# Two of sixteen weight loads cut into 24, 24 and 80 rows, with two eight-row transfers in between

## The chip, the core and the metric

The kernel runs on one core of one Trainium2 chip. TensorE (PE) multiplies matrices and transposes, VectorE (DVE) and ScalarE (ACT) work on vectors, GpSimd (POOL) and SyncE (SP) mostly issue transfers. Transfers from the chip's main memory (HBM) into the core's memory (SBUF) are moved by 16 DMA engines that all queues share. The metric is the time of one execution on the device in microseconds (us), the median of several executions.

## The reference

Two stages. First an attention over 4 batches, 8 heads, 768 positions and 64 columns a head; three heads see all earlier positions, five see the first 4 positions and a window of 64. Then a mixture of experts with soft slots: 32 slots take weighted means of all 3072 rows of the attention's result, 8 experts with two weight matrices each (512 x 1024 and 1024 x 512) work on four slots each, and every row gets a weighted mean of the slots' results.

```python
x = attn_out.transpose(0, 2, 1, 3).reshape(B * S, H * D)   # 3072 x 512
logits = x @ phi                                           # 3072 x 32
slot_input = softmax(logits, over rows).T @ x              # 32 x 512
for e in range(8):
    h = relu(slot_input[e] @ w1[e])                        # 4 x 1024
    slot_out[e] = h @ w2[e]                                # 4 x 512
out = softmax(logits, over slots) @ slot_out
```

## The kernel before

**Loads.** q, k and v of the four batches and the 16 weights (numbers 0 to 7 are w1 of the experts, 8 to 15 are w2) are read from HBM as 4-byte numbers and written to SBUF as 2-byte numbers, a conversion made by the transfer itself. All of these loads are issued by POOL, through `dma` (lines 329 to 337), and stand in its one queue, q0. A load of q, k or v of batches 1 to 3 (`load_part`, line 347) has 96 rows, each of two 4 KB pieces as written; one of a weight (`load_w`, line 385) has 128 rows, each of two 4 KB pieces. Batch 0 is loaded in halves (384 KB each), weights 14 and 15 in column halves (`load_half`, line 381). The order of the calls is the order of the queue: batch 0, w0, batch 1, w1, w2, batch 2, w3 to w5, batch 3, w6 to w10 (lines 516 to 525), later w11 to w13 and the halves 14.0, 15.0, 14.1, 15.1 (lines 859 to 866). In the views of the transfers, the row of a load gives the KB that it writes and the us from issue to landing.

**Memory for the loads.** Eleven slots (`slots`, line 246) take q, k, v and the weights 0 to 10. A slot in which a q, k or v lay is free again when TensorE has transposed it (line 566); a weight stays. The weights 11 to 15 go to memory that the attention no longer needs.

**The order of the work.** The program is laid out by a list scheduler (`Plan`, lines 33 to 149). Every operation has its engine, an estimated duration, what it depends on, the buffers that it takes and frees, and a due time (its key); the planner repeatedly takes the operation that can start first, and the one with the lowest key among those within 0.12 us of it. `SHIFTS` (line 167) is a list of changes of due times for the operations between two keys; the loads, with key -100, are not among them. Instructions of an engine run in the planned order. The issue of a load is an operation on POOL; it waits for the issue before it and, by lines 330 and 331, for the landing of the eighth load before it. The estimated landing is an operation on a made-up engine called DMA. POOL also makes a few tables, and three copies of exponentials (`EL4`, line 801), each of which a transpose on TensorE (line 836) waits for.

**The attention.** For each of the 16 pairs of batch and head group, TensorE transposes q, k and v (line 566), forms scores (line 599), ScalarE takes exponentials (line 668), VectorE applies masks (line 615), TensorE multiplies by v (line 729), and the result is normed (line 750), transposed again (line 762) and used for the logits.

**The experts.** From about 115 us on, TensorE multiplies the slots' means by the weights 0 to 7 (line 904), then the results by the weights 8 to 15 (line 942). The last two, 14 and 15, are used by column halves: halves 14.0 and 15.0 complete the left half of the slots' results, whose rows of the output are formed (line 998), scaled (lines 1006 and 1008) and stored (line 1017) while 14.1 and 15.1 still load; with these the right half follows, and the last stores.

**What the change touches.** `load_w` for the weights 6 and 7 (called at line 525), and the memory of `ident_u` (line 261), a 96 x 96 matrix that the transposes of batch 0 use.

Of the kernel before, what the change touches and what calls it, by code (L numbers as in the profile page):

```python
# [11 lines left out]
BF16 = mybir.dt.bfloat16  # L12
# [3 lines left out]
PSUM = bass.MemoryType.PSUM  # L16
KB = 512
PAD = 16


class Buf:
# [194 lines left out]
def kernel(  # L216
# [14 lines left out]
    P = 128  # L231
# [3 lines left out]
    NS = moe_phi.shape[1]  # L235
# [4 lines left out]
    sb = ctx.enter_context(tc.tile_pool(name="sb", bufs=1))  # L240
# [4 lines left out]

    slots = [sb.tile([P, 8 * KB + 2 * PAD], BF16, name=f"slot{i}") for i in range(11)]
    qk_mem = [sb.tile([P, 12 * KB], BF16, name=f"qk{i}") for i in range(2)]
# [10 lines left out]
    ssum = sb.tile([P, B], F32, name="ssum")  # L258
    fmx = sb.tile([P, 4, 2, 4, 66], BF16, name="fmx")
    ident = sb.tile([P, P], BF16, name="ident")  # L260
    ident_u = sb.tile([96, 96], BF16, name="ident_u")
    ident_r = sb.tile([P, P], BF16, name="ident_r")
    phf = sb.tile([P, 4, NS], F32, name="phf")
    phi = sb.tile([P, 4, NS], BF16, name="phi")
# [50 lines left out]
    def on(eng, occ, late=0.18):  # L315
        return {eng: (occ, occ + late)}
# [12 lines left out]
    def dma(name, nbytes, buf, dst, src, deps=()):  # L329
        if len(chain) >= 8:  # L330
            deps = list(deps) + [chain[-8]]
        iss = pl.op("issue " + name, on("POOL", 0.645, 1.4), -100, deps=list(deps) + [fifo[0]],
                    acq=[buf] if buf else [], lead=1.3, emit=lambda o: nc.gpsimd.dma_start(dst(), src))  # L333
        fifo[0] = iss
        took = nbytes / 425000.0
        chain.append(pl.op("land " + name, {"DMA": (took, took + 1.3 + min(2.1, 0.22 * len(chain)))}, -100, deps=[iss] + chain[-1:], lead=3.4))
        return chain[-1]
# [25 lines left out]
    wbuf = [Buf("S8") for _ in range(NW)]  # L363
    wland = [None] * NW
    late_mem = {}

    def w_mem(i):

        m = late_mem[i]() if i in late_mem else slots[wbuf[i].slot][:, :]
        return m.rearrange("p (h x) -> p h x", h=2)[:, :, 0:4 * KB]  # L370
# [14 lines left out]
    def load_w(i, deps=()):  # L385
        if i < NE:
            src = moe_w1[i].rearrange("(di h a) f -> di h (a f)", h=2, a=2)
        else:
            src = moe_w2[i - NE].rearrange("(fi h a) d -> fi h (a d)", h=2, a=4)
        wland[i] = dma(f"w{i}", 2 << 20, None if i in late_mem else wbuf[i],  # L390
                       lambda: w_mem(i), src, deps=deps)


    def tables(o):
# [32 lines left out]
    def head_flags(o, n):  # L427
        cp = nc.scalar.copy if o.eng == "ACT" else nc.gpsimd.tensor_copy
        for a, j0, j1 in ((1, 1, 4), (0, 0, 1)):
            cp(fmx[:, n, :, j0:j1, :].rearrange("p i j d -> p i (j d)"),  # L430
               thr[:, a, n::4].rearrange("p (i o) -> p i o", o=1).to_broadcast([P, 2, 66 * (j1 - j0)]))
# [72 lines left out]
    for n in range(4):  # L504
        o_fm[n] = pl.op(f"fm{n}", on("ACT", 0.65) if n == 0 else on("POOL", 0.9), -8 if n == 0 else T * n - 3.5,
                        deps=[o_fl], emit=lambda o, n=n: head_flags(o, n))
# [5 lines left out]
    def batch_loads(b):  # L512
        for x in "qkv":
            load_part(x, b)

    load_w(0)
    batch_loads(1)
    load_w(1)
    load_w(2)
    batch_loads(2)  # L520
    for i in (3, 4, 5):
# [67 lines left out]
    def evs(x, b, n):  # L589
        return ev[x, 0, n // 2] if b == 0 else ev[x, b]  # L590
# [15 lines left out]
    def mask_emit(b, n, g):  # L606
        def f(o):
            pT = pTs[PTb[b, n].slot]
            mh = msk[:, n::4, :]
            if g < 2:  # L610
                pT = pT[:, :, 1024 * g:1024 * (g + 1)].rearrange("p i (a c) -> p i a c", a=2)[:, :, :, 0:256]
                mh = mh[:, :, 256 * g:256 * g + 512].rearrange("p i (a c) -> p i a c", a=2)
            else:
                pT, mh = pT[:, :, 2048:2432], mh[:, :, 256:640]
            nc.vector.tensor_tensor(pT, pT, mh, op=ALU.mult)  # L615
        return f
# [5 lines left out]
    for b in range(B):  # L622
        for n in range(4):
# [29 lines left out]
            for kk, g in enumerate(range(5)):  # L653
# [19 lines left out]
                for m, gs in enumerate(MGROUPS):  # L673
                    if gs[-1] == g:
                        o_m = pl.op(f"MK.{p}.{m}", on("DVE", [0.605, 0.605, 0.47][m]), key + 0.3,
                                    deps=[expo[p, x] for x in gs] + [o_hm[n]], emit=mask_emit(b, n, m))
# [3 lines left out]
        for ns in ([(0, 1), (2, 3)] if b == 0 else [(0, 1, 2, 3)]):  # L680
            sc = Buf("SC")

            def emit_lx(o, b=b, sc=sc, ns=ns):
# [4 lines left out]
                      deps=list(dict.fromkeys(e for n in ns for x in "qk" for e in evs(x, b, n))),  # L688
# [14 lines left out]
    for b in range(B):  # L703
        for n in range(4):
# [5 lines left out]
            for i in iorder:  # L710
                deps, need = [v2e[p], vfo[p]], set()
# [7 lines left out]
                def emit_pv(o, b=b, n=n, p=p, i=i):  # L719
                    pT = pTs[PTb[b, n].slot]  # L720
                    vb = vbs[VBb[b].slot]
                    for h in range(2):
                        for j in range(i + 1):
# [3 lines left out]
                            else:  # L727
# [5 lines left out]
                             deps=list(dict.fromkeys(deps)) + ([last] if last else []),  # L733
# [8 lines left out]
            for i0, i1 in halves:  # L742
                part = f"{p}" if i1 - i0 == 6 else f"{p}.{i0}"

                def emit_nm(o, i0=i0, i1=i1, b=b, n=n, p=p):
# [9 lines left out]
                                 deps=[pvo[i1 - 1], XBb[b].op], acq=[XBb[b]] if n == 0 else [], rel=[PVb[p]],  # L755
# [94 lines left out]

    late_mem[11] = lambda: qk_mem[QTb[2].slot][:, 0:8 * KB + 2 * PAD]
    late_mem[12] = lambda: vx_mem[VBb[2].slot][:, 0:8 * KB + 2 * PAD]
    late_mem[13] = lambda: xv_mem[:, 0:8 * KB + 2 * PAD]
    late_mem[14] = lambda: pt_mem[:, 10 * KB * PTb[3, 2].slot:10 * KB * PTb[3, 2].slot + 8 * KB]
# [233 lines left out]
```

## Time and profile before

| | us |
|---|---|
| time, median of 3 executions | 150.83 (150.63 to 150.85) |
| the profiled execution's own time | 150.88 |
| its span (first to last instruction) | 149.1 |
| TensorE busy | 125.5 |
| VectorE busy | 109.1 |
| ScalarE busy | 107.4 |
| POOL busy | 33.1 |

The profile is of one execution. Its times count from the start of the span; the execution's own time holds the 1.8 us around the span as well. A row of the timeline gives start, duration, engine, line, the tile that is written and what is read, and in brackets how long the engine had been idle before and what ended that. In the slices of the span a digit is the busy share of a fortieth in tenths. The DMA share of a window is the mean number of transfers' pieces in progress per DMA engine, which exceeds 1 where pieces overlap on one engine.

### The profile page before, as it was taken

How to read it: one execution, taken by the hardware profiler on the slowest of the kernel's cores; microseconds unless marked ns; L12 is line 12 of the kernel's file. 1: busy time of each engine (PE TensorE's matmuls, PEld its weight loads, DVE VectorE, ACT ScalarE, POOL GpSimd, SP SyncE). 2: the span in 40 equal slices, each digit the busy share in tenths (PEclk: the TensorE clock that was granted, in tenths of full speed). 3: DMA queues.
4: the chain of work that ended last, by engine and by line, in shares of the span. 5: the costliest groups of instructions: out<-in, count | busy, mean ns of one | idle time of the engine just before them, and what ended most of it. 6: DMA issues, size and time to landing. Idle time of an engine off the chain costs nothing.

```text
span 149.1 us, 5309 instructions
## 1 busy us (share of the span) xinstructions
PE 125.5 (84%) x2351; PEld 85.8 (58%) x2351; DVE 109.1 (73%) x232; ACT 107.4 (72%) x138; POOL 33.1 (22%) x58
## 2 busy tenths in 40 slices
PE   6799987996999999999999997999779994959100
PEld 1297665774776776877667775757565552634000
DVE  1897999966898988999899997998953130749500
ACT  3127899996779999999999997999913530738300
POOL 6996301111111001210210122050630000430000
PEclk9999999999599999999999999999968999586975
DMA  2999999999999999999999999999999999999995
GB/s 21 193 210 210 216 214 215 216 214 213 216 210 215 215 216 218 209 212 218 214 216 212 211 216 219 216 211 212 213 220 215 201 196 198 142 305 336 391 422 209
DMA packets 14263, 32.92 MB, mean 221 GB/s; under 512 B 1376, under 2 KB 7008, under 8 KB 13856
## 3 DMA queue, kind: packets, MB, share of 16 engines
q0 software_dynamic: 11536, 27.79, 95.0%
q1 hardware_dynamic: 2704, 4.79, 8.5%
q8 instruction: 18, 0.29, 0.7%
q14 instruction: 5, 0.04, 0.1%
HBM read 52.50 MB, written 6.29 MB: 394 GB/s over the span
## 4 chain that ended last, share of the span: by engine, by line
PE 48%; DMA 15%; DVE 11%; ACT 8%; issue 7%; POOL 3%; DVEq 1%; POOLq 0%; ACTq 0%
DMA qk<-in_moe_w_dram 15%; PE tr L566 13%; PE sc L599 11%; PE pv L729 11%; ACT pt L668 5%; PE tr L762 3%; PE bk L998 3%; DVE xv L750 2%; PE tr L632 2%; DVE pt L615 2%; PE sc L485 2%; DVE vx L322 1%; ACT qk L320 1%; DVE slot L1008 1%; DVE vf L647 1%
## 5 line engine op out<-in xcount | busy, mean ns | idle before, releaser
L668 ACT ACTIVATE pt<-sc 128x1024 bf16<-128x1024 f32 x80 | 77.4, 1047 | 4.9 <-PE sc L599 4.6
L599 PE MATMUL sc<-qk 64*128 64x128 bf16 (+3 forms) x288 | 32.1, 298 | 1.6 <-ACT pt L668 1.4
L615 DVE TENSOR_TENSOR pt<-pt,msk 128x1024 bf16<-128x1024 bf16 (+1 forms) x48 | 30.1, 639 | 1.5 <-ACT pt L668 1.1
L729 PEld LDWEIGHTS <-pt 128*128 128x128 bf16 x640 | 23.9, 98 | 6.8 <-issue 3.7
L729 PE MATMUL pv<-vx,pt 128*128 128x65 bf16 x352 | 26.9, 194 | 0.1
L566 PEld LDWEIGHTS <-slot 96*64 96x64 bf16 x768 | 20.1, 115 | 7.2 <-issue 5.3
L729 PE MATMUL pv<-vf,pt 128*128 128x65 bf16 x288 | 21.7, 196 | 0.9 <-DVE xv L750 0.9
L566 PE MATMUL tr<-ident,slot 96*64 96x96 bf16 x576 | 18.0, 212 | 1.3 <-issue 1.3
L322 DVE COPY qk<-tr 128x768 bf16<-128x768 bf16 x28 | 14.9, 549 | 4.0 <-PE tr L566 3.9
L599 PEld LDWEIGHTS <-qk 64*128 64x128 bf16 x288 | 11.5, 95 | 9.0 <-issue 3.3
L750 DVE TENSOR_TENSOR xv<-pv,rs 128x768 bf16<-128x768 f32 (+1 forms) x17 | 15.5, 910 | 0.6
L333 POOL DMA_DIRECT2D slot<-in_moe_w_dram x11 | 7.8, 707 | 26.6 <-PE tr L566 19.2
L1006 ACT ACTIVATE slot<-bk,rrow 128x256 f32<-128x256 f32 (+1 forms) x17 | 8.5, 548 | 3.6 <-PE bk L998 3.5
L762 PE MATMUL tr<-ident,xv 128*128 128x128 bf16 x96 | 8.8, 230 | 1.4 <-DVE xv L750 0.9
L1008 DVE TENSOR_SCALAR slot<-bk,rrow 128x256 f32<-128x256 f32 (+1 forms) x19 | 9.3, 561 | 0.6 <-PE bk L998 0.4
L762 PEld LDWEIGHTS <-xv 128*128 128x128 bf16 x96 | 6.2, 102 | 4.9 <-DVE xv L750 2.5
L632 PE MATMUL tr<-ident,xv 128*128 128x128 bf16 x96 | 8.2, 220 | 1.0 <-issue 0.9
L322 DVE COPY xT<-tr 128x768 bf16<-128x768 bf16 (+1 forms) x14 | 7.3, 525 | 2.3 <-PE tr L762 1.3
L998 PE MATMUL bk<-msk,expT 128*128 128x256 bf16 (+1 forms) x36 | 8.4, 413 | 0.7 <-DVE msk L983 0.7
L322 DVE COPY vx<-tr 128x768 bf16<-128x768 bf16 x13 | 7.1, 550 | 1.1 <-PE tr L632 1.0
L632 PEld LDWEIGHTS <-xv 128*128 128x128 bf16 x96 | 5.7, 97 | 3.0 <-issue 2.5
L1017 POOL DMA_DIRECT2D out_dram<-slot x4 | 2.8, 709 | 19.6 <-DVE slot L1008 19.5
(101 smaller groups left out, 152.1 us busy)
## 6 DMA issues: line engine op xcount, KB each, us to landing
slot<-in_moe_w_dram POOLq DMA_DIRECT2D x11, 1024.0 KB, 26.4
out_dram<-slot SPq DMA_DIRECT2D x3, 1024.0 KB, 6.6
slot<-in_q_dram POOLq DMA_DIRECT2D x3, 768.0 KB, 30.4
slot<-in_k_dram POOLq DMA_DIRECT2D x3, 768.0 KB, 32.7
slot<-in_v_dram POOLq DMA_DIRECT2D x3, 768.0 KB, 23.8
out_dram<-slot SPq DMA_DIRECT2D x3, 512.0 KB, 3.7
qk<-in_moe_w_dram POOLq DMA_DIRECT2D x1, 1024.0 KB, 21.3
vx<-in_moe_w_dram POOLq DMA_DIRECT2D x1, 1024.0 KB, 24.0
```

What stands on the lines that cost most here:

```text
L322: nc.vector.tensor_copy(dst, src)
L566: nc.tensor.transpose(dst_, rv[:, i, 8 * c + s, :], idv)
L599: nc.tensor.matmul(scb[sc.slot][:, i, c:c + 128 * nb], kk, qq.rearrange("p b c -> p (b c)"), start=True, stop=True)
L615: nc.vector.tensor_tensor(pT, pT, mh, op=ALU.mult)
L632: nc.tensor.transpose(t[:, 128 * j:128 * (j + 1)], vT[:, 6 * n + j, :], ident)
L668: nc.scalar.activation(pTs[PTb[b, n].slot][:, :, 512 * g:512 * (g + 1)], scb[sc.slot], ACT.Exp, scale=scale)
L729: nc.tensor.matmul(pvb[:, h, 65 * i:65 * (i + 1)], lt, rhs, start=(j == 0), stop=(j == i))
L750: nc.vector.tensor_tensor(xo, pvw[:, :, :, 0:64], r.rearrange("p i (j o) -> p i j o", o=1).to_broadcast([P, 2, i1 - i0, 64]), op=ALU.mult)
L762: nc.tensor.transpose(t[:, 128 * i:128 * (i + 1)], xv[:, i, 128 * n:128 * (n + 1)], ident)
L998: nc.tensor.matmul(banks[bf.slot][:, 0:w], out_lhs(gi, r), slot_out[:, cs], start=True, stop=True)
L1006: nc.scalar.activation(d, banks[bf.slot][:, 0:w], ACT.Copy, scale=sc_)
L1008: nc.vector.tensor_scalar(d, banks[bf.slot][:, 0:w], sc_, None, op0=ALU.mult)
```

## The change

The loads of the weights 6 and 7 are each cut into three, of rows 0 to 23, 24 to 47 and 48 to 127, into the same memory as before. After each of the first two a small transfer is issued: eight rows of 32 numbers from the slots' matrix `phi`, into eight rows of SBUF that nothing else uses. There are four such transfers, each with eight rows of its own, in rows 96 to 127 of a tile that has been made taller for that; rows 0 to 95 hold what `ident_u` held. Two transfers on POOL's queue thus become ten, in the order 24 rows, small, 24 rows, small, 80 rows, for weight 6 and then for weight 7. The first part of a weight takes the slot; all parts go through `dma`, so each of the ten counts for the rule of the eighth load before.

```diff
--- before.py
+++ after.py
@@ -16,6 +16,7 @@
 PSUM = bass.MemoryType.PSUM
 KB = 512
 PAD = 16
+UNEVEN = {6: (24, 0, 24, 0, 80), 7: (24, 0, 24, 0, 80)}
 
 
 class Buf:
@@ -258,7 +259,9 @@
     ssum = sb.tile([P, B], F32, name="ssum")
     fmx = sb.tile([P, 4, 2, 4, 66], BF16, name="fmx")
     ident = sb.tile([P, P], BF16, name="ident")
-    ident_u = sb.tile([96, 96], BF16, name="ident_u")
+    ident_m = sb.tile([P, 96], BF16, name="ident_u")
+    ident_u = ident_m[0:96, :]
+    few = [ident_m[96 + 8 * x:104 + 8 * x, 0:NS] for x in range(4)]
     ident_r = sb.tile([P, P], BF16, name="ident_r")
     phf = sb.tile([P, 4, NS], F32, name="phf")
     phi = sb.tile([P, 4, NS], BF16, name="phi")
@@ -387,8 +390,19 @@
             src = moe_w1[i].rearrange("(di h a) f -> di h (a f)", h=2, a=2)
         else:
             src = moe_w2[i - NE].rearrange("(fi h a) d -> fi h (a d)", h=2, a=4)
-        wland[i] = dma(f"w{i}", 2 << 20, None if i in late_mem else wbuf[i],
-                       lambda: w_mem(i), src, deps=deps)
+        if i not in UNEVEN:
+            wland[i] = dma(f"w{i}", 2 << 20, None if i in late_mem else wbuf[i],
+                           lambda: w_mem(i), src, deps=deps)
+            return
+        rows, p0 = UNEVEN[i], 0
+        for x, n in enumerate(rows):
+            if n == 0:
+                dma(f"gap{i}.{x}", 1024, None, lambda m=few.pop(): m, moe_phi[0:8, :])
+                continue
+            wland[i] = dma(f"w{i}.{p0}", n << 14, wbuf[i] if p0 == 0 else None,
+                           lambda p0=p0, n=n: w_mem(i)[p0:p0 + n], src[p0:p0 + n], deps=deps)
+            p0 += n
+        assert p0 == 128
 
 
     def tables(o):
```

## The prediction

> **What bounds the kernel now.** I read the page first, then the chain that ended last, then POOL's timeline, then the landing of single transfers, then the last microseconds of the loads in short windows.
>
> ```profile
> span 149.1 us, 5309 instructions
> ...
> PE 125.5 (84%) x2351; PEld 85.8 (58%) x2351; DVE 109.1 (73%) x232; ACT 107.4 (72%) x138; POOL 33.1 (22%) x58
> ...
> DMA  2999999999999999999999999999999999999995
> ...
> q0 software_dynamic: 11536, 27.79, 95.0%
> ...
> q8 instruction: 18, 0.29, 0.7%
> ...
> PE 48%; DMA 15%; DVE 11%; ACT 8%; issue 7%; POOL 3%; DVEq 1%; POOLq 0%; ACTq 0%
> ```
>
> TensorE is the busiest engine, but the row to look at is DMA: from the second slice on, the 16 engines are always nine tenths busy or more, nearly all with POOL's queue q0. The chain says where that becomes the end:
>
> ```profile
> 107.56 0.86 POOL pt L333
> 108.43 23.09 DMA qk<-in_moe_w_dram
> 131.56 0.43 PE bk L942 x8
> ```
>
> The last load (second half of weight 15) is issued at 108.43 and lands at 131.5, behind everything queued ahead of it; TensorE starts on it at once. TensorE had to wait there, and before for the first half:
>
> ```profile
> 126.30 0.55 PE L942 MATMUL bk<-qk,xT 128*32 128x256 bf16 x8 [2.03 <-DMA qk<-in_moe_w_dram]
> ...
> 131.56 0.40 PE L942 MATMUL bk<-qk,xT 128*32 128x256 bf16 x8 [1.17 <-DMA qk<-in_moe_w_dram]
> ```
>
> So the time is: end of the load stream at 131.5, plus a fixed tail of 149.1 - 131.5 = 17.6 us, plus 150.88 - 149.1 = 1.8 us outside the span. A later stream costs one to one; an earlier one pays up to about 2.0 us, until TensorE itself is the last (the waits of 2.03 and 1.17 are on consecutive parts of one chain and both move with the stream).
>
> Where the stream ends is not the same for all engines. The last columns of the windows are clock, DMA share and GB/s:
>
> ```profile
> 124.00:127.00 3.00, 0.97 (x28) 0.43 (x17) 0.00 (x0) 0.12 (x1) 0.00 (x0) 0.90 1.45 197
> 127.00:128.00 1.00, 1.00 (x25) 0.84 (x23) 0.31 (x1) 0.36 (x1) 0.00 (x0) 0.50 1.17 165
> 128.00:129.00 1.00, 1.00 (x7) 0.72 (x5) 0.99 (x3) 0.94 (x3) 0.21 (x1) 0.50 0.78 100
> 129.00:130.00 1.00, 1.00 (x9) 0.50 (x8) 1.00 (x4) 1.00 (x3) 0.90 (x2) 0.58 0.70 114
> ```
>
> From 128 on, half the rate is left (100 of 197): about eight engines have finished, eight work on to 130 and 131.5. So there are **early and late engines**, 2 to 3.5 us apart. The q8 row gives a likely cause: 18 instruction fetches take 0.7% of 16 x 149.1 us = 16.7 us, 0.93 us each; shared by eight engines that is 2.1 us per engine. Even engines would end the stream sooner: the rate lost in 127 to 130 is 32 + 97 + 83 = 212 KB, 1.1 us at 197 KB/us, and at most about as much again after 130. This spread is what the change can touch: how many rows each engine gets.
>
> **The change part by part.** (1) The bytes of weights 6 and 7 stay the same. (2) Two transfers become ten on q0: eight more, four of them eight rows of 32 numbers. (3) POOL issues eight more. (4) The eight-back rule (line 330: an issue waits for the landing of the eighth transfer before it) now counts pieces. (5) The 24-row parts can be uneven over the 16 engines. The small rows go to memory that nothing reads.
>
> *Cost of a transfer in the stream (2).* Landings come from issue time plus time to landing. For the seven loads from weight 6 to 13:
>
> ```profile
> 59.87 0.70 POOL L333 DMA_DIRECT2D slot<-in_moe_w_dram  x1
> ...
> 98.72 0.71 POOL L333 DMA_DIRECT2D xv<-in_moe_w_dram  x1 [0.33 <-PE tr L810]
> ```
> ```profile
> slot<-in_moe_w_dram POOLq DMA_DIRECT2D x1, 1024.0 KB, 25.7
> ```
> ```profile
> xv<-in_moe_w_dram POOLq DMA_DIRECT2D x1, 1024.0 KB, 21.1
> ```
>
> 59.87 + 25.7 = 85.57 and 98.72 + 21.1 = 119.82: 34.25 / 7 = 4.89 us for 128 rows, 0.61 us per row of an engine (eight rows each). For 96 rows, the q and v of batch 1 (issued 7.97 and 9.23, two transfers apart):
>
> ```profile
> 7.97 0.66 POOL L333 DMA_DIRECT2D slot<-in_q_dram  x1
> ...
> 9.23 0.66 POOL L333 DMA_DIRECT2D slot<-in_v_dram  x1
> ```
> ```profile
> slot<-in_q_dram POOLq DMA_DIRECT2D x1, 768.0 KB, 17.6
> ```
> ```profile
> slot<-in_v_dram POOLq DMA_DIRECT2D x1, 768.0 KB, 23.8
> ```
>
> 25.57 and 33.03: 3.73 us for six rows each. From 8r + f = 4.89 and 6r + f = 3.73, f = 0.25 us per transfer; but if the time went by rows alone (4.89 / 8 = 0.611 against 3.73 / 6 = 0.622) f is 0 to 0.07. A single fetch of 0.93 us between two landings explains the difference, so I bound f by 0 and 0.15 (no reason lets an added transfer take less than nothing) and take 0.08, nearer to the proportional pair: 8 x 0.08 = **0.64 us**, bounds 0 and 1.2. All engines get this, the late ones too, and nothing hides it.
>
> [...]
>
> *POOL and the eight-back rule (3, 4).*
>
> ```profile
> 12.99 0.72 POOL L333 DMA_DIRECT2D slot<-in_moe_w_dram  x1
> ...
> 33.55 0.70 POOL L333 DMA_DIRECT2D slot<-in_moe_w_dram  x1 [2.96 <-PE tr L566]
> 38.43 0.66 POOL L333 DMA_DIRECT2D slot<-in_q_dram  x1 [4.18 <-PE sc L599]
> 43.39 0.63 POOL L333 DMA_DIRECT2D slot<-in_k_dram  x1 [4.30 <-DMA slot<-in_moe_w_dram]
> ...
> 59.25 0.63 POOL L333 DMA_DIRECT2D slot<-in_v_dram  x1 [10.85 <-PE tr L566]
> ...
> 71.71 0.83 POOL L801 COPY elg<-elg 128x576 bf16<-128x576 bf16 x1 [6.91 <-DMA slot<-in_q_dram]
> ...
> 88.39 0.70 POOL L333 DMA_DIRECT2D slot<-in_moe_w_dram  x1 [4.94 <-PE tr L566]
> ```
> ```profile
> slot<-in_moe_w_dram POOLq DMA_DIRECT2D x1, 1024.0 KB, 29.8
> ```
> ```profile
> slot<-in_moe_w_dram POOLq DMA_DIRECT2D x1, 1024.0 KB, 36.1
> ```
> ```profile
> slot<-in_q_dram POOLq DMA_DIRECT2D x1, 768.0 KB, 35.1
> ```
> ```profile
> slot<-in_v_dram POOLq DMA_DIRECT2D x1, 768.0 KB, 21.4
> ```
>
> The rule is seen at 43.39: weight 2, eighth before k of batch 3, landed at 12.99 + 29.8 = 42.79, and the issue follows 0.60 us later. Eight issues at 0.70 are 5.6 us more of POOL. Now the new order: the third part of weight 6 (80 rows) is eighth after weight 5, which lands at 33.55 + 36.1 = 69.65: issued 70.25 to 70.95. The copy at 71.71 (line 801, which really waits for ScalarE's exponentials, not for the q named) comes next, so it is not delayed, by a margin of 0.76 us; behind it stands the transpose of line 836 on TensorE. Weight 7's first part waits for q of batch 3 (38.43 + 35.1 = 73.53), its second for v (59.25 + 21.4 = 80.65): issued at 81.25; the small transfer behind that for weight 6's first part, some 1.3 us after v, so about 82.6; its third part at 83.3, weights 8 and 9 at 84.0 and 84.7, before 88.39, where weight 10 waits for a buffer as now. I take the order of all other instructions as unchanged, since each added operation finds POOL idle.
>
> Does the stream run dry meanwhile? When v lands at 80.65, weight 6 (4.9 us) and 24 rows of weight 7 (0.9 us) are queued: the late engines have work to 86.5. The third part of weight 7 is issued at 83.3; if it takes 2.5 us to start (an upper bound from the 8 KB load of line 454, whole 2.5 us to landing) it is there at 85.8. So nothing is lost on late engines; the early ones, 2 to 3 us ahead, may idle up to 2 us, which the spread at the end covers. Without that cover every microsecond is paid.
>
> ```profile
> ri<-in_is_retrieval_dram SPq DMA_DIRECT2D x1, 8.0 KB, 2.5
> ```
>
> *Which engines get the rows (5).* No row shows a transfer on POOL's queue other than 96 or 128 rows, both even over 16. Bounds, at 0.61 us a row: the late engines give away two rows of 32 (below) and the stream ends 1.22 us earlier; or they get two more and it ends 1.22 us later. I take the value between, 0, from those two nearest rows: a row is two 4 KB pieces, 24 rows are 48 = 3 x 16 pieces, and over four such parts any dealer that moves on comes round evenly.
>
> [...]
>
> Sum: 150.88 + 0.64 = **151.5** (0 from POOL, 0 from uneven rows). The median shown is 150.83, 0.05 below the profiled execution.
>
> **Rivals.** *Faster: the early engines take more.* If rows are dealt one by one, 16 to a round, 24 rows are a round and a half and the eight small rows fill the half: every 24-row part then starts at the same engine. Eight engines get two rows and eight get one, four times: 8 against 4, where even is 6. If the eight are the early ones, the late ones end 1.22 us sooner: 150.88 - 1.22 + 0.64 = 150.3. For it: 24 + 8 = 32 closes the round exactly, and half the engines are late, with about four rows' time (2.4 us) between the halves. Against: nothing says which half starts.
>
> *Slower: the late engines take more.* The same deal from the other half, or a deal that always begins at the first engine with two rows for each of 12: late engines are then among those with eight rows, 150.88 + 1.22 + 0.64 = 152.7. It decides as soon as one of the latest engines lies in the favoured set. [...]
>
> *Eight engines with three rows each.* With a fixed start these have 6 rows too many, 3.7 us: on the early ones they become the last, about 151.9; on the late ones 155.2.
>
> *Queue or copy.* If parts wait for one another, or weight 5 lands over 0.76 us later, POOL stands still in front of line 801 and the stream dries: 153 and more. Against: the two loads of line 457 go to different rows of one tile, and both are issued within 1.41 us, though each takes 3.9 us to land.
>
> ```profile
> 1.17 1.41 SPq L457 DMA_DIRECT2D phf<-in_moe_phi_dram  x2
> ```
> ```profile
> phf<-in_moe_phi_dram SPq DMA_DIRECT2D x2, 32.0 KB, 3.9
> ```
>
> *No difference*: f near 0 and rows even, 150.9.
>
> **How the numbers follow.** Even rows 0.42 (own range 150.9 to 152.1 by the bounds of f; 0.04 of it within 0.2%), late engines 0.24, early engines 0.20 (0.03 of it within 0.2%), eight engines 0.05, queue 0.04, no difference 0.05. Faster by over 0.2% (about 0.3 us, what a measurement of this kernel can tell): 0.17; within: 0.04 + 0.03 + 0.05 = 0.12; slower: 0.38 + 0.24 + 0.05 + 0.04 = 0.71. The range 150.2 to 152.9 reaches over the first three cases and leaves out the eight-engine and queue cases and the edges.
>
> **What would show it.** Right: the second half of weight 15 lands at about 132.2, its 23.1 us grown by 0.6; the rate still halves near 128.6; line 801 starts near 71.7; the tail stays 17.6 us. Rows even or not is seen in the windows before the last landing: if the rate holds at 197 up to the end, the early engines took more; if it halves earlier and the last landing is near 133.4, the late ones did. Wrong: a wait in front of line 801, DMA shares under 1.0 between 80 and 90, or a gap of 4 us between landings that the small transfers cause.

## The result and the profile after

The changed kernel takes 151.74 us, median of 20 executions (151.1 to 152.86); the kernel before took 151.0 beside it (20 executions, 150.63 to 151.93). The ratio is 1.0044, interval 1.0027 to 1.006: **0.66 us slower**, between 0.41 and 0.91. The forecast was 151.5, or 0.64 more. The size came out nearly as forecast, but not by the way that the forecast gave for it: as far as the number goes, that is luck.

The profiled execution took 151.65 us. The lines of the page of the changed kernel that answer to those of before:

```profile
span 149.9 us, 5320 instructions
...
PE 123.4 (82%) x2351; PEld 83.3 (56%) x2351; DVE 110.3 (74%) x232; ACT 107.8 (72%) x138; POOL 37.4 (25%) x66
...
DMA  2999999999999999999999999999999999997994
...
q0 software_dynamic: 11792, 27.79, 94.8%
...
q8 instruction: 18, 0.29, 0.7%
```

POOL has eight instructions more (66 for 58) and is busy 4.3 us more; q0 moves the same 27.79 MB in 256 more pieces. The other engines have their old counts. The order of all instructions other than these issues is the same on each engine. In the text of the changed kernel the lines of `dma` and of the attention stand 3 to 14 lower: 333 is now 336, 801 is 815, 942 is 956.

The end of the chain that ended last, and TensorE's rows on the last load, in the changed kernel:

```profile
107.24 0.87 POOL pt L336
108.11 23.71 DMA qk<-in_moe_w_dram
131.86 0.64 PE bk L956 x7
```
```profile
126.23 0.40 PE L956 MATMUL bk<-qk,xT 128*32 128x256 bf16 x8 [2.23 <-DMA qk<-in_moe_w_dram]
...
131.86 0.61 PE L956 MATMUL bk<-qk,xT 128*32 128x256 bf16 x8 [1.80 <-DMA qk<-in_moe_w_dram]
```

The bound is the same as before: TensorE waits 1.80 us for the second half of weight 15. That half lands 23.71 us after its issue at 108.11, at 131.82: **0.30 us later than before**, where the forecast had 0.6. From TensorE's start on it to the end of the span are 149.9 - 131.86 = 18.0 us, where before they were 149.1 - 131.56 = 17.5. So of the 0.77 us between the two profiled executions, 0.30 are the stream and **0.47 the tail**, which the forecast took as fixed. These are two single executions; what the tail does in the median isn't shown.

POOL's timeline of the changed kernel (start, duration, engine, line, transfer; in brackets the idle time before and what ended it):

```profile
57.68 0.61 POOL L336 DMA_DIRECT2D slot<-in_moe_w_dram  x1
58.28 0.54 POOL L336 DMA_DIRECT2D ident_u<-in_moe_phi_dram  x1
58.82 0.61 POOL L336 DMA_DIRECT2D slot<-in_moe_w_dram  x1
63.69 0.52 POOL L336 DMA_DIRECT2D ident_u<-in_moe_phi_dram  x1 [4.26 <-DMA slot<-in_moe_w_dram]
69.70 0.64 POOL L336 DMA_DIRECT2D slot<-in_moe_w_dram  x1 [5.49 <-DMA slot<-in_moe_w_dram]
70.33 0.68 POOL L815 COPY elg<-elg 128x576 bf16<-128x576 bf16 x1
73.66 0.60 POOL L336 DMA_DIRECT2D slot<-in_moe_w_dram  x1 [2.64 <-PE tr L580]
77.07 0.53 POOL L336 DMA_DIRECT2D ident_u<-in_moe_phi_dram  x1 [2.81 <-DMA slot<-in_k_dram]
81.36 0.60 POOL L336 DMA_DIRECT2D slot<-in_moe_w_dram  x1 [3.76 <-DMA slot<-in_v_dram]
82.29 0.52 POOL L336 DMA_DIRECT2D ident_u<-in_moe_phi_dram  x1 [0.32 <-DMA slot<-in_moe_w_dram]
82.80 2.20 POOL L336 DMA_DIRECT2D slot<-in_moe_w_dram  x3
88.33 0.70 POOL L336 DMA_DIRECT2D slot<-in_moe_w_dram  x1 [3.33 <-PE tr L580]
```

This is the plan of the forecast nearly to the tenth: 69.70 for a forecast 70.25, 81.36 for 81.25, 82.29 for 82.6, 88.33 for 88.39. The copy (line 815) isn't delayed. Weight 7, one issue at 64.09 before, now has five, from 73.66 to 82.80, because of the rule of the eighth load before, which now counts pieces.

The rates while weights 6 and 7 move (last columns: granted clock, DMA share, GB/s), before and after:

```profile
76.00:80.00 4.00, 4.00 (x100) 2.93 (x100) 3.94 (x8) 3.64 (x5) 0.70 (x1) 1.00 1.07 216
80.00:84.00 4.00, 4.00 (x98) 2.87 (x93) 3.85 (x8) 4.00 (x5) 0.71 (x1) 1.00 1.07 216
84.00:88.00 4.00, 4.00 (x114) 3.20 (x110) 3.87 (x9) 4.00 (x6) 0.00 (x0) 1.00 1.06 213
88.00:92.00 4.00, 3.09 (x58) 2.07 (x54) 3.63 (x7) 3.63 (x5) 2.10 (x3) 1.00 1.07 216
```
```profile
76.00:80.00 4.00, 3.96 (x92) 2.74 (x88) 3.79 (x8) 3.62 (x5) 0.53 (x1) 1.00 1.06 211
80.00:84.00 4.00, 4.00 (x90) 2.93 (x90) 3.92 (x9) 3.87 (x5) 2.31 (x4) 1.00 1.08 208
84.00:88.00 4.00, 3.43 (x98) 2.62 (x96) 3.33 (x7) 3.73 (x5) 0.85 (x2) 1.00 1.06 204
88.00:92.00 4.00, 3.37 (x61) 2.35 (x60) 3.59 (x7) 3.53 (x5) 2.10 (x3) 1.00 1.07 215
```

Before, the rate hardly moves. After, 208 and 204 stand between 80 and 88: 4 x (8 + 9) = 68 KB less, 0.32 us at 213 KB/us, just where the queue lives on pieces issued at 81.36 to 82.80. From 88 on the rate is back. The 211 for 216 between 76 and 80 stands in several kernels below with no piece issued late (210 to 214 there), so 5 GB/s in one window is no more than their scatter.

### The profile page after: what moved, and what is told of

It reads as the page before. It is cut to its first block, busy times and chain, and to the rows that moved or that the text cites. A ratio compares the mean times of both kernels' runs of the same rounds, so it can differ in the third digit from the quotient of the medians.

```text
span 149.9 us, 5320 instructions
## 1 busy us (share of the span) xinstructions
PE 123.4 (82%) x2351; PEld 83.3 (56%) x2351; DVE 110.3 (74%) x232; ACT 107.8 (72%) x138; POOL 37.4 (25%) x66
## 3 DMA queue, kind: packets, MB, share of 16 engines
q0 software_dynamic: 11792, 27.79, 94.8%
## 4 chain that ended last, share of the span: by engine, by line
DMA 39%; PE 37%; DVE 9%; issue 3%; POOL 3%; ACT 2%; DVEq 1%; POOLq 0%
DMA slot<-in_q_dram 23%; DMA qk<-in_moe_w_dram 16%; PE tr L580 9%; PE pv L743 8%; PE sc L613 8%; PE bk L1012 4%; PE tr L776 3%; PE sc L499 2%; DVE pt L629 1%; DVE xv L764 1%; PE tr L646 1%; ACT qk L323 1%; DVE vx L325 1%; POOL slot L336 1%; DVE slot L1022 1%
## 5 line engine op out<-in xcount | busy, mean ns | idle before, releaser
L743 PEld LDWEIGHTS <-pt 128*128 128x128 bf16 x640 | 23.4, 97 | 6.9 <-issue 3.7
L580 PEld LDWEIGHTS <-slot 96*64 96x64 bf16 x768 | 19.3, 112 | 8.4 <-issue 5.0
L743 PE MATMUL pv<-vf,pt 128*128 128x65 bf16 x288 | 21.2, 194 | 0.9 <-DVE xv L764 0.9
L336 POOL DMA_DIRECT2D slot<-in_moe_w_dram x15 | 10.1, 673 | 24.4 <-DMA slot<-in_v_dram 6.5
L776 PE MATMUL tr<-ident,xv 128*128 128x128 bf16 x96 | 8.2, 220 | 1.3 <-DVE xv L764 0.9
L646 PE MATMUL tr<-ident,xv 128*128 128x128 bf16 x96 | 8.2, 220 | 0.7 <-issue 0.6
L776 PEld LDWEIGHTS <-xv 128*128 128x128 bf16 x96 | 5.8, 97 | 4.4 <-DVE xv L764 1.9
L661 DVE TENSOR_TENSOR vf<-vx,fmx 128x528 bf16<-128x528 bf16 x16 | 7.7, 492 | 0.4
```

The source lines that it names most:

```text
L580: nc.tensor.transpose(dst_, rv[:, i, 8 * c + s, :], idv)
L646: nc.tensor.transpose(t[:, 128 * j:128 * (j + 1)], vT[:, 6 * n + j, :], ident)
L743: nc.tensor.matmul(pvb[:, h, 65 * i:65 * (i + 1)], lt, rhs, start=(j == 0), stop=(j == i))
L776: nc.tensor.transpose(t[:, 128 * i:128 * (i + 1)], xv[:, i, 128 * n:128 * (n + 1)], ident)
```

## The experiments

**Theories.** *Count* (the forecast): each added transfer costs every engine about 0.08 us, wherever it stands. *Rows*: the cost is an uneven deal of the 24-row parts over the engines. *Late issue*: the transfers as such are nearly free, but pieces that wait for the eighth piece before them are issued so late that engines run out of work between 82 and 88 us. All kernels below differ from the changed one in `UNEVEN` (rows of each part of a weight; 0 stands for a small transfer) and in `few`, the memory of the small transfers. A difference below is the ratio's, applied to the kernel before as it was measured beside that run (medians 151.1 to 151.2); the plain difference of the two medians departs from it by up to 0.2 us.

*Splits alone.*
```diff
-UNEVEN = {6: (24, 0, 24, 0, 80), 7: (24, 0, 24, 0, 80)}
+UNEVEN = {6: (24, 24, 80), 7: (24, 24, 80)}
```


> The change without its four small transfers: weights 6 and 7 as 24, 24 and 80 rows, four more transfers than before. By the count of transfers (0.08 us each): +0.3 us. By the queue (the late issues of POOL from 81 us on, which came from ten pieces in the eight-back rule, leave engines without work; here the last part is issued at about 73 and weight 8 at 77): +0.0 to +0.2 us.

Measured: 151.16, ratio 0.9998 (0.9979 to 1.0016), -0.03 us for four added transfers.

*Even parts, same count and order.*
```diff
+UNEVEN = {6: (32, 0, 32, 0, 64), 7: (32, 0, 32, 0, 64)}
```


> The change with 32, 32 and 64 rows in place of 24, 24 and 80: the same ten transfers, every part a multiple of 16 rows. By the count of transfers, and by the queue alike (issues from 81 us on as late as in the change): +0.6 us. If the uneven rows are what costs: +0.2 or less.

Measured: 151.54, ratio 1.0023 (1.0009 to 1.0038), +0.35 us: about half of the change's cost, with nothing uneven.

*Splits of four weights, with no, one and two small transfers each.* These ask how rows are dealt: a deal that always starts at the same engine would send four parts too many to it, and small transfers would shift a start that moves.
```diff
+UNEVEN = {i: (24, 24, 80) for i in range(6, 10)}
```


> Weights 6 to 9 as 24, 24 and 80 rows, no small transfers: eight more transfers than before. The theory (rows come out even over the 16 engines, each added transfer takes 0.08 us of every engine): +0.6 us, 151.5. Always the lowest twelve engines with two rows each: they get 4 rows too many (eight parts, half a row each), 2.4 us, so about +3.1 us. Rows dealt one by one: two parts close three rounds, even, +0.6. Twelve engines from a start that moves: one weight favours one half, the next the other, even, +0.6.

Measured: 151.44, ratio 1.0028 (1.0006 to 1.0051), +0.42 us for eight added.
```diff
+UNEVEN = {i: (24, 24, 0, 80) for i in range(6, 10)}
```


> Weights 6 to 9 as 24, 24, a small transfer of eight rows, 80: twelve more transfers. The theory: +1.0 us, rate halves before the end as before. Twelve engines from a start that moves by the engines used: 12 + 12 + 8 = 32, so the same eight engines get a row more and the other eight a row less in each of four weights, 4 rows or 2.4 us each way: about -0.5 to +1 if the early ones take more (they become the last), +3.4 if the late ones do. Rows dealt one by one: even over two weights, +1.0. Always the lowest twelve: +3.4.

Measured: 151.48, ratio 1.0025 (1.0 to 1.0049), +0.38 us for twelve added.
```diff
+UNEVEN = {i: (24, 0, 24, 0, 80) for i in range(6, 10)}
```


> The change's own pattern on four weights, 6 to 9, sixteen more transfers. The theory: twice the change, +1.3 us. Rows dealt one by one from the first engine: eight engines get 4 rows more than even, eight 4 rows less, 2.4 us each way: -0.5 to +1 if the early ones take more, +3.7 if the late ones do. Twelve engines from a moving start: even over two weights, +1.3. Always the lowest twelve: +3.7.

Measured: 152.0, ratio 1.0059 (1.0032 to 1.0085), +0.89 us for sixteen added. (The one profile of this kernel is of an execution of 153.86 us, 1.9 us above its median, and isn't read here; the 176 to 185 GB/s in the expectation of the sixteen even ones are from it.) A deal that always starts at the same engine would give half or more of the engines four rows too many over the eight parts, 4 x 0.61 = 2.4 us on the late ones or as much off them. None of the three shows that, so the rival of fixed starts falls.

*Small transfers alone.*
```diff
+UNEVEN = {i: (0, 0, 128) for i in range(6, 10)}
```


> Weights 6 to 9 whole, two small transfers ahead of each: eight more transfers, no uneven rows. The theory, by which the count alone matters: +0.6 us. If the small transfers are nearly free and the cost is that of the parts: 0. If the small ones are what costs (0.17 us each): +1.4.

Measured: 151.28, ratio 0.9998 (0.9979 to 1.0018), -0.03 us for eight added. At 0.08 us each it would be +0.64; the upper end of the interval is +0.27, 0.03 each (the medians, 151.28 against 151.11, give +0.17, 0.02 each). *Count*, as one price for every added transfer, falls.

*One half of the engines, and the other.* Small transfers of 24 rows stand in for those of eight. If each transfer of 24 rows goes to twelve engines and the next begins where it ended, the parts of the first kernel give one half of the engines eight rows where even is six, and those of the second give them to the other half.
```diff
+UNEVEN = {6: (24, 24, 80), 7: (0, 0, 128), 8: (24, 24, 80), 9: (0, 0, 128)}
+    few = [ident_m[96:120, NS * y:NS * (y + 1)] for y in range(4)]
```


> Weights 6 and 8 as 24, 24 and 80 rows, and two small transfers of 24 rows of 32 numbers ahead of weights 7 and 9: eight more transfers. If 24 rows go to twelve engines from a start that moves by twelve, the two parts of a weight give eight engines one row more and the others one less, and the two small ones of 24 bring the start back, so that weight 8 favours the same eight: 2 rows, 1.22 us each way. With the early engines favoured the stream ends 1.2 us sooner, -1.2 to -0.6 us with the cost of eight transfers; with the late ones favoured +1.2 to +1.8. Rows even (the start does not move, or pieces are dealt singly): +0.4, as with eight parts on four weights.

Measured: 151.35, ratio 1.0005 (0.999 to 1.002), +0.08 us.
```diff
+UNEVEN = {6: (0, 0, 128), 7: (24, 24, 80), 8: (0, 0, 128), 9: (24, 24, 80)}
+    few = [ident_m[96:120, NS * y:NS * (y + 1)] for y in range(4)]
```


> The same with the small transfers ahead of weights 6 and 8, and weights 7 and 9 cut: the other half of the engines favoured. By the moving start the opposite sign of the run before it, 2.4 us away from it: +1.2 to +1.8 where that is faster, -1.2 to -0.6 where that is slower. Rows even: +0.4, the same in both.

Measured: 151.7, ratio 1.0037 (1.0017 to 1.0057), +0.56 us. The latest engines lie in one half or in both, so at least one of the two should be two rows, 1.22 us, slower; neither is (the second one's interval ends at +0.86), and they differ by 0.48. *Rows*, as a sum over the engines, falls too. Why the second is slower isn't settled. It matters for *late issue*: this kernel costs nearly what the change does, yet its rate stays at 210 GB/s or more in every 4 us from 80 to 96, and all its transfers are issued 6.9 us or more before the first engine is through with what stands ahead of them (2.4 us in the change).

*Sixteen added, all even.*
```diff
+UNEVEN = {i: (32, 0, 32, 0, 64) for i in range(6, 10)}
```


> Weights 6 to 9 as 32, 32 and 64 rows with two small transfers each: the sixteen added transfers of the run that put the change's pattern on four weights (+0.9 us), as late issues, but every part a multiple of 16 rows. By the count of transfers (0.04 us each, the slope over the runs so far): +0.65 us, and +0.9 like the uneven one if the late issues alone starve the engines. If it takes late issues and uneven rows together: about +0.4 to +0.65, and the rate of the loads between 80 and 96 us stays at 210 GB/s or more, where the uneven pattern on four weights fell to 176 to 185.

Measured: 151.56, ratio 1.0017 (0.9998 to 1.0037), +0.26 us for sixteen: 0.016 us each. In its profile the rate falls to 201 GB/s between 84 and 88 and to 203 between 88 and 92, with rows that are all even.

*The same ten transfers, with two whole weights between.* Weight 9 is cut in place of weight 7, so the late pieces have two weights queued ahead of them.
```diff
+UNEVEN = {6: (24, 0, 24, 0, 80), 9: (24, 0, 24, 0, 80)}
```


> The change with weight 9 in place of weight 7: the same ten transfers and parts, but two whole weights lie between the cut ones, so that the eight-back rule no longer makes POOL issue late. By the count of transfers: +0.3 us. By rows or by small transfers between uneven parts: +0.66 like the change. By the late issues: +0.3 or less, with the early engines' finish less than 0.5 us later than before the change (0.9 in the change).

Measured: 151.27, ratio 1.0008 (0.9989 to 1.0028), +0.12 us. POOL's timeline of it shows weights 7 and 8 whole, and the parts of weight 9 at the end:

```profile
73.70 0.70 POOL L336 DMA_DIRECT2D slot<-in_moe_w_dram  x1 [2.26 <-DMA slot<-in_q_dram]
77.41 0.71 POOL L336 DMA_DIRECT2D slot<-in_moe_w_dram  x1 [3.01 <-PE sc L613]
81.97 0.61 POOL L336 DMA_DIRECT2D slot<-in_moe_w_dram  x1 [3.84 <-PE tr L580]
82.61 0.52 POOL L336 DMA_DIRECT2D ident_u<-in_moe_phi_dram  x1
83.12 0.60 POOL L336 DMA_DIRECT2D slot<-in_moe_w_dram  x1
```

Weight 8, ahead of these parts, lands on its first engine at 92.2, about 10 us after the issue of the first. In the changed kernel the second part of weight 7 was issued at 81.36, when the first engine had only the rest of weight 6 (until 82.80) and 24 rows ahead of it. The windows of this kernel, weights 7 and 8 apart:

```profile
80.00:84.00 4.00, 4.00 (x93) 2.96 (x90) 3.82 (x9) 4.00 (x5) 1.85 (x4) 1.00 1.08 214
84.00:88.00 4.00, 3.78 (x102) 2.76 (x99) 3.69 (x8) 3.90 (x6) 1.20 (x3) 1.00 1.05 213
```

The loss of 80 to 88 is gone.

*One weight alone.*
```diff
+UNEVEN = {6: (24, 24, 80)}
```


> Weight 6 alone as 24, 24 and 80 rows, no small transfers. If 24 rows go to twelve engines from a start that moves, eight engines get one row more and eight one less: the early and the late ones shift by 0.6 us against each other, the end moves by -0.5 or +0.7 us (or by one in some executions and the other in the rest, if the start is carried over). If rows are dealt evenly in each weight: +0.1 us and no shift.

Measured: 150.92, ratio 0.9997 (0.9973 to 1.0021), -0.05 us; its interval (-0.41 to +0.32) holds no change and neither of the two shifts.

*The change again, beside the last three.*

> The change itself once more, for a second profile: +0.66 us in the median. If the early engines ran out of work in it, the rate between 80 and 88 us is again below 210 GB/s and the early engines finish about 0.9 us later; if that was chance, 213 GB/s. The tail behind the last landing is 19.35 us when TensorE's clock is back at full by 130 us, 19.85 us when it is at half, in this kernel as in the others.

Measured: 151.82, ratio 1.0059 (1.0034 to 1.0084), +0.89 us. Its windows:

```profile
80.00:84.00 4.00, 4.00 (x91) 2.93 (x89) 3.92 (x9) 3.81 (x5) 2.05 (x4) 1.00 1.09 212
84.00:88.00 4.00, 3.42 (x98) 2.65 (x94) 3.33 (x7) 3.73 (x5) 1.10 (x2) 1.00 0.99 181
88.00:92.00 4.00, 3.36 (x64) 2.32 (x59) 3.67 (x8) 3.54 (x5) 2.10 (x3) 1.00 1.06 213
```

Here the hole is deeper: 4 x (213 - 181) = 128 KB, 0.60 us, with the DMA share at 0.99, the lowest of all these windows. Between 85 and 86 it is 0.90, so here engines stood idle for part of the time. In the first profile of the change that isn't seen: its share between 84 and 88 is 1.06, as before the change, and the loss lies in pieces that take longer (below). The even kernel with the same ten transfers, issued at the same times within 0.4 us, has no such hole:

```profile
80.00:84.00 4.00, 4.00 (x91) 2.93 (x89) 3.93 (x9) 3.96 (x5) 2.04 (x4) 1.00 1.06 210
84.00:88.00 4.00, 3.43 (x98) 2.66 (x94) 3.32 (x7) 3.73 (x5) 1.05 (x2) 1.00 1.08 211
```

Two things may account for the difference: two parts of 32 rows leave one row more for each engine (16 rows, 0.61 us) in the queue while the 64-row part is on its way than two of 24; and no engine goes without rows, if they are dealt evenly. In a part of 24 rows some do: in the changed kernel the two engines that are last with weight 6 land it at 85.94 and 86.00, and all have landed weight 7's first part by 86.35, at most 0.41 us later, where one row takes 0.61. Of the 16 landings of that part four come at 83.59 to 84.20 and twelve from 84.67 on; in the kernel with splits of four weights four at 83.56 to 84.00 and twelve from 84.95 on. Twelve engines with two rows and four with none fit this. That is an estimate from these landings; no view counts the rows of an engine.

The trace also holds the landing of each load on the 16 engines, and the duration of each 4 KB piece (0.324 us as a rule). From one execution of each kernel; "weight 10" is the mean landing of the first load behind all cut ones, against before; the lead is the time from the issue of a transfer to the moment when the first engine is through with the transfer ahead of it, the shortest of those of the weights 6 to 9:

| kernel | added | difference, us | lead, us | weight 10, us | last load, mean landing, us | last landing | pieces over 0.5 us, begun 82 to 92 |
|---|---|---|---|---|---|---|---|
| before | | | 9.8 | (103.74) | 129.23 | 131.52 | 1 |
| the change | 8 | +0.66 | 2.4 | +0.38 | 129.88 | 131.82 | 7 |
| the change again | 8 | +0.89 | 2.3 | +0.77 | 130.34 | 131.86 | 12 |
| even, two weights | 8 | +0.35 | 2.7 | +0.16 | 129.41 | 131.76 | 1 |
| small alone | 8 | -0.03 | 6.4 | +0.10 | 129.33 | 131.55 | 1 |
| weights 6 and 9 | 8 | +0.12 | 9.2 | +0.26 | 129.49 | 131.58 | 1 |
| splits of four | 8 | +0.42 | 7.1 | +0.20 | 129.43 | 131.83 | 1 |
| one half | 8 | +0.08 | 5.8 | +0.38 | 129.62 | 131.58 | 2 |
| the other half | 8 | +0.56 | 6.9 | +0.54 | 129.77 | 131.62 | 1 |
| one small, four | 12 | +0.38 | 3.0 | +0.22 | 129.46 | 132.06 | 2 |
| even, four weights | 16 | +0.26 | 2.4 | +0.70 | 129.94 | 131.57 | 10 |
| splits of two | 4 | -0.03 | 9.8 | +0.25 | 129.48 | 131.82 | 1 |
| one weight | 2 | -0.05 | 7.3 | +0.06 | 129.30 | 131.06 | 0 |

The mean landing tells how late the 16 engines are in the mean; ahead of the cut weights it already differs by up to 0.16 us from kernel to kernel. The six kernels with eight added transfers and at most two long pieces lose 0.10 to 0.54 us by the last load: mean 0.28, **0.01 to 0.07 us each**. The change loses 0.65 and 1.11. Of that, 0.38 and 0.77 are there at weight 10; the other 0.27 and 0.33 come only behind weight 12, some 25 us after the cut weights, and no run tells why. At weight 10 only the second of its two profiles is later than the kernels without long pieces (up to 0.54). Seven or more pieces over 0.5 us are seen only in the change and with sixteen even ones (the longest 1.24, 1.37 and 1.58 us): where the shortest lead is 2.3 to 2.4 us, and not where it is 2.7 us or more. That needs no uneven rows, since the sixteen are all even. So for the stream *late issue* is borne out, by one or two profiles of each kernel. In the change the long ones but one begin between 83.2 and 87.6 us, behind the issues of 81.36 to 83.06; what they exceed 0.324 us by is 0.23 us for each of 16 engines in the first profile and 0.31 in the second. Why a piece takes longer there isn't shown.

The last landing is another matter: it stands at +0.30 and +0.34 for the change, but at +0.30 for the splits of two as well, which cost nothing in the median, and at +0.05 for sixteen even ones in spite of a mean of +0.71. So there the spread of the engines covers the loss. All of this is against one execution of the kernel before, of 150.88 us, 0.1 to 0.3 us under the medians that it had beside these runs.

## Why the prediction was right, and where its steps failed

**The bound** held: the last landing sets the end, and POOL, TensorE's order and the copy of line 801 are not in it.

**The term of added transfers was mis-sized.** It was 8 x 0.08 = 0.64 us for every engine, wherever the transfers stand. No one price fits the runs: eight added transfers cost -0.03 to +0.56 us where no more than two pieces are long, 0.25 in the mean or 0.03 each; sixteen even ones +0.26; small ones alone at most 0.03 each. Of the two readings, the proportional one (0 to 0.07) was the nearer. The forecast's sum came out by luck: this term was too high, and a loss that was set at nothing made up for it.

**The step that failed is the loss of the late issues, set at nothing.** The forecast found their times (81.25, 82.6, 83.3) and that the early engines might run dry; it set their loss at nothing since "the spread at the end covers" it. The rates show a loss between 80 and 88 us, 68 KB in one execution and 128 KB in the other. Moving the second cut weight away took it out of the rates, and most of the cost out of the time (+0.12 for +0.66 and +0.89, with intervals that do not overlap for the repeat: 1.0008 with at most 1.0028, against 1.0059 with at least 1.0034). So where the same ten transfers stand decides most of their cost. The long pieces go with the shortest leads, even rows or not, which is what late issues would do. That this loss is the whole cost in time is argued and not shown: sixteen even ones lose as much by weight 10 (0.70) and cost +0.26, and the second of the mirrored pair costs +0.56 with a lead of 6.9 us and no hole. How the loss got past the cover isn't shown either: the last landing moved by 0.30 and 0.34, no more than in the splits of two, which cost nothing.

**Its own signs.** The last load landed at 131.82 and not at 132.2, the tail was 18.0 and not 17.6 us. Of the signs of being wrong, the DMA share under 1.0 between 80 and 90 came in the repeat (0.99), not in the first profile; there was no wait in front of the copy.

**Rows even** held: in a part twelve engines get two rows and four none, by the estimate from the landings, but by the times the sum over four parts is even (the mirrored pair differs by 0.48 us, not by the 2.4 of two rows each way). The rivals with early engines (150.3), late engines (152.7) and eight engines (151.9 and 155.2) fall with the mirrored pair, the four-weight kernels and the landings (twelve engines, not eight, by the same estimate).

**The tail was not fixed.** It is 17.5 us in some profiles and 18.0 in others. Windows of the tail in the kernel before and the changed one (granted clock third from the end of the row):

```profile
126.00:129.00 3.00, 2.70 (x40) 1.91 (x40) 1.29 (x4) 1.41 (x4) 0.21 (x1) 0.57 1.14 155
129.00:132.00 3.00, 1.80 (x22) 0.82 (x20) 1.47 (x4) 1.61 (x4) 2.63 (x4) 0.86 0.78 210
132.00:135.00 3.00, 2.37 (x13) 1.63 (x14) 2.53 (x7) 1.94 (x5) 0.00 (x0) 0.71 0.98 335
135.00:138.00 3.00, 3.00 (x11) 1.18 (x10) 2.90 (x6) 2.58 (x5) 0.00 (x0) 0.72 0.96 333
```
```profile
126.00:129.00 3.00, 2.61 (x43) 1.95 (x43) 1.55 (x5) 1.73 (x5) 0.47 (x1) 0.85 1.31 176
129.00:132.00 3.00, 1.20 (x15) 0.46 (x17) 1.20 (x4) 1.04 (x3) 2.36 (x4) 0.50 0.92 236
132.00:135.00 3.00, 2.34 (x17) 1.31 (x10) 1.91 (x5) 1.05 (x3) 0.00 (x0) 0.50 0.98 343
135.00:138.00 3.00, 3.00 (x11) 1.32 (x9) 2.60 (x6) 2.55 (x5) 0.00 (x0) 0.50 0.67 233
```

In the changed kernel TensorE's clock stays at half through the last part of the matmuls (0.50 from 129 to 138 us); before, it came back to full within the tail (full from 129.8 to 133.2 us and again from 136.7; 0.86, 0.71 and 0.72 in these windows). The small-alone kernel had the long tail (149.6 - 131.59 = 18.0) and a median of -0.03, so a long tail in the one profile does not go with a slower median; how often each of the two comes in each kernel isn't known, and part of any difference of 0.3 us here may be that.

**Left open:** why the second of the mirrored pair costs 0.56 and the first 0.08; why the four-weight splits cost 0.4 with no hole; what delays the change's last loads behind weight 12; and whether even parts cost less than uneven ones in the same place (+0.35 with at most 1.0038, against +0.66 with at least 1.0027: the intervals overlap). A kernel with the same ten pieces and no rule of eight, the direct test of late issue, was not tried.

## What to carry to other kernels

Cutting a queued transfer into pieces costs little in the stream (0.01 to 0.07 us each here, by the mean landing); what can cost more is what the pieces do to a rule that counts transfers, and here the place of the pieces made 0.1 us into 0.7 to 0.9. Before adding pieces, work out when the last of them may be issued and how many bytes are then queued on the engine that is furthest ahead, not on the latest one. A spread between engines may cover a loss or not: with sixteen even ones 0.05 of a mean of 0.71 us reached the last landing, in the change 0.30 of 0.65. Set it as a bound of the range and not at nothing.

## What was not expected of the hardware

The time from TensorE's start on the last load to the end has only two values in thirteen profiled executions: 17.5 to 17.6 us (before, splits of two and of four, weights 6 and 9, one weight) and 18.0 (the other eight), some 0.5 us apart, by whether the granted clock of TensorE is at full between 130.5 and 132.6 us. The clock's steps there are about 3.4 us or a multiple of it apart (before: half from 126.4, full from 129.8, half from 133.2, full from 136.7; the changed kernel: half from 128.1 to 138.3, three times 3.4). What sets where they fall, and so which of the two values an execution has, isn't shown.

A small transfer of eight rows behind another transfer in the queue lands 0.18 to 0.21 us after it in the changed kernel, in the mean of the 16 engines, yet eight of them alone moved the mean landing of the last load by 0.10 us in all. Why these two differ isn't shown.
